# FFN1 a batch later and in groups of 512 tokens, with u through DRAM, in a fused attention and squared-ReLU FFN kernel

## The chip, the cores and the metric

The kernel runs on one core of one Trainium2 chip. The metric is the device time of one execution in microseconds. Three runs of the kernel before took 1504.96, 1505.45 and 1505.6 us; the median, 1505.45 us, is the time that the change is measured against.

## The reference

Attention over 8 batches of 12 heads, with RMS-normed q and k, feeds a two-layer feed-forward network (FFN). All of it is float32 at the interface; w_in and w_out arrive as float64.

```python
q_n, k_n = rmsnorm(q, g_q), rmsnorm(k, g_k)          # q, k, v: 8 x 12 x 448 x 64
scores = (q_n @ k_n.T) / 8
attn = softmax(scores)
x = (attn @ v)                                       # laid out as 3584 tokens x 768
h = x @ w_in                                         # 768 x 2048
r = max(h, 0)
out = (s * r * r + b) @ w_out                        # 2048 x 768
```

A float32 product of full accuracy is made on TensorE out of float32r parts: a number is split into a high part (what float32r keeps) and the rest, and three products high*high, high*low and low*high are added in PSUM.

## The kernel before

**Work and slots.** Two heads make a pair, 48 pairs in all, 6 to a batch. Attention is laid out over 384 slots, 8 to a pair: slot s makes the transposed scores of chunk s (`score_t`: two matmuls, L406 and L409), the exponentials of the same chunk (ScalarE), the plain scores of chunk s + 10 (`score`, L368) with their maximum (`maximum`, L379, VectorE), and the product with the values of chunk s - 2 (`weigh`, L465). A negative slot number is the run-in: the program begins at slot -22. Everything else hangs on the slots in a table, `jobs`: `at(s, f, ...)` puts a step into slot s. Inside a slot every engine gets its instructions in the order of the code, and each engine works through its own list in order. So the table sets the order, and a late instruction holds back all that stands behind it on its engine. SyncE (SP) issues all DMAs, in order too, and a DMA that must wait holds back those behind it.

**Two ways to prepare a pair.** The 6 pairs of batch 0 come in by rows: `load_rows`, `norm_rows` (ScalarE squares, L234 on VectorE sums, GpSimd makes the inverse root, L238, and scales the rows, L239), `turn` (TensorE transposes into PSUM, L246) and `split_turned` (three copies on ScalarE, two subtractions on VectorE, L258 and L259). The other 42 pairs come in already transposed (`load_kq`), and the inverse roots go through DRAM (`load`, `norm`, `keep`, `spread`); `scale` and `split_kq` then take 2 GpSimd multiplications or subtractions of 64 or 128 partitions more per half pair (L330, L352, L353) and L310 and L331 on VectorE. Pairs below `NV` (12) take the value product in plain float32 (one matmul, two passes in the trace); the others split the exponentials (`split_e`, ScalarE; `split_e_lo`, L446, VectorE) and take three float32r matmuls, or two for the last chunk of four.

**After a pair.** `take` copies the product out, `gather` (DMA) collects the row sums, `invert` (VectorE, L488) inverts them, `divide` steps 1 and 2 spread them through DRAM, and step 3 multiplies on GpSimd (L506) into u, at slot 8p + 18 for pair p. Six u tiles stay in SBUF until the batch is whole.

**FFN1.** w_in is converted from float64 in 24 pieces of 128 x 512 (`convert`: L126, L129, L131 and L134 on VectorE, L127 and L137 on ScalarE, L140 on GpSimd). `PACE` starts them at slots -18, -14, -10, -6, -2, 2 and then every fifth slot up to 91. From slot 61 on the `filler` puts 6 FFN1 matmuls into each slot, between the attention's own: 16 blocks of 128 features x 18 matmuls of 448 tokens for each batch (`ffn_in`, L181). Every 48 slots the next batch begins, and just before that `split_x` splits its six u tiles into x, two in each of three slots (L514 on ScalarE, L515 on VectorE). The x tiles are single, so the split has to wait until the last block of the batch before has read them. The relu goes to DRAM (`r_d`). Batches 0 to 6 are filled into the attention; batch 7 runs after it, at the head of the end part, beside the conversion of w_out (32 pieces, VectorE and ScalarE).

**FFN2.** The end part squares r, splits it and runs 28 tiles of 128 tokens x 96 matmuls of 384 columns (`ffn_out`, L706). Its first three tiles take turns while w_out is still being converted.

## Time and profile before

| what | value |
|---|---|
| median of three runs | 1505.45 us |
| the profiled execution: span | 1504.4 us |
| the three runs: lowest and highest | 1504.96 and 1505.6 us |
| TensorE clock granted, mean | 0.988 |
| instructions in the span | 21397 |
| bytes moved by DMA | 230.83 MB |

The span of the profiled execution, from the first to the last instruction, is 1.05 us under the median of the runs; sums are made against the span, and 1.05 us is added at the end. In the lines of the profile PE is TensorE's matmuls and PEld its weight loads, DVE is VectorE, ACT ScalarE, POOL GpSimd, SPq the DMA issues of SyncE. An entry as `ph<-x,wih` reads: writes tile ph, reads x and wih (buffer numbers left out). A group's line ends in busy us, mean ns of one instruction, and the engine's idle time just before such instructions with what ended it.

### The profile page before, as it was taken

Reading aid. Unit: us, or ns where it says so; the run is one execution under the profiler, and the core shown is the slowest. Engines: PE = TensorE matmul, PEld = TensorE weight load, DVE = VectorE, ACT = ScalarE, POOL = GpSimd, SP = SyncE. Lnnn points to the kernel's source line nnn. Section 1 sums busy time; section 2 is a strip of 40 time slices with the busy share of each in tenths; the row PEclk is TensorE's granted clock in tenths of the full one; section 3 lists DMA queues with packets and bytes.
Section 4 is the critical chain, followed back from the end, with each engine's and each line's share of the span. In section 5 each row is a group of like instructions: output and inputs, shape, how many; then the busy total and the mean of one; then the engine's idle time right before and its main releaser. Section 6 shows DMA issues by size and latency. Waiting matters only on the chain.

```text
span 1504.4 us, 21397 instructions
## 1 busy us (share of the span) xinstructions
PE 1452.9 (97%) x7344; PEld 1330.3 (88%) x7344; DVE 874.7 (58%) x1319; ACT 786.3 (52%) x1436; POOL 689.9 (46%) x569
## 2 busy tenths in 40 slices
PE   6887899999999999999999999999999999999998
PEld 6555688899899889889989989999999999999998
DVE  6998876766766676676676665289532222222210
ACT  3675555766766766766676676446432222222210
POOL 6589888777677677777777764100000000000000
PEclk8898999999999999999999999999999999999999
DMA  4468776566566666666656652188333233223200
GB/s 140 110 180 230 214 234 190 167 198 193 175 196 190 193 175 194 191 190 191 183 168 195 191 173 91 67 295 255 113 105 78 80 101 90 78 87 100 84 22 32
DMA packets 221916, 230.83 MB, mean 153 GB/s; under 512 B 78896, under 2 KB 199728, under 8 KB 221808
## 3 DMA queue, kind: packets, MB, share of 16 engines
q1 hardware_dynamic: 221808, 229.47, 51.8%
q8 instruction: 58, 0.95, 0.3%
q14 instruction: 50, 0.41, 0.1%
HBM read 177.21 MB, written 40.84 MB: 145 GB/s over the span
## 4 chain that ended last, share of the span: by engine, by line
PE 88%; DVE 5%; DMA 3%; issue 1%; ACT 1%; POOL 1%; SPq 0%; DVEq 0%; POOLq 0%; ACTq 0%
PE po L706 31%; PE ph L181 30%; PE av L465 13%; PE st L406 4%; PE st L409 4%; PE sh L368 4%; DVE x L515 2%; PE warmth L272 1%; DVE nmx L379 1%; DMA zt<-uz 1%; DMA z_d<-zt 1%; DMA rb<-i_d 0%; DVE al L446 0%; DVE wai L134 0%; DVE wai L129 0%
## 5 line engine op out<-in xcount | busy, mean ns | idle before, releaser
L181 PE MATMUL ph<-x,wih 128*128 128x448 f32 x1536 | 490.9, 367 | 2.6 <-DVE x L515 2.2
L181 PEld LDWEIGHTS ph<-x,wih 128*128 128x128 f32 x1536 | 289.0, 188 | 33.6 <-issue 6.4
L379 DVE TENSOR_REDUCE nmx<-sh 112x1 fp32r<-112x448 f32 x384 | 236.6, 619 | 136.0 <-PE sh L368 130.9
L181 PE MATMUL ph<-x,wil 128*128 128x448 f32 x768 | 294.1, 383 | 0.0
L425 ACT ACTIVATE st<-st 128x448 f32<-128x448 f32 (+1 forms) x288 | 151.1, 525 | 220.8 <-PE st L409 204.2
L706 PE MATMUL po<-woh,gh 128*128 128x384 f32 x896 | 228.0, 334 | 0.0
L706 PE MATMUL po<-wol,gh 128*128 128x384 f32 x896 | 228.0, 334 | 0.0
L706 PE MATMUL po<-woh,gl 128*128 128x384 f32 x896 | 227.7, 334 | 0.0
L368 PE MATMUL sh<-ka,qa 128*112 128x448 f32 x384 | 147.1, 385 | 30.5 <-ACT wih L137 12.5
L465 PE MATMUL av<-ah,vs 128*128 128x448 f32 x576 | 164.3, 366 | 0.1
L406 PE MATMUL st<-qa,ka 128*128 128x448 f32 (+1 forms) x384 | 163.5, 426 | 0.5 <-ACT e L421 0.5
L706 PEld LDWEIGHTS po<-woh,gh 128*128 128x128 f32 x896 | 161.7, 188 | 0.4 <-ACT r L198 0.3
L706 PEld LDWEIGHTS po<-wol,gh 128*128 128x128 f32 x896 | 161.8, 188 | 0.0
L706 PEld LDWEIGHTS po<-woh,gl 128*128 128x128 f32 x896 | 161.8, 188 | 0.0
L181 PEld LDWEIGHTS ph<-x,wil 128*128 128x128 f32 x768 | 144.4, 188 | 17.8 <-issue 6.9
L433 ACT CAST ah<-st 128x448 fp32r<-128x448 f32 (+1 forms) x288 | 154.1, 535 | 1.8
L446 DVE TENSOR_TENSOR al<-st,ah 128x448 fp32r<-128x448 f32 x216 | 132.1, 611 | 35.6 <-ACT ah L433 21.7
L368 PEld LDWEIGHTS sh<-ka,qa 128*112 128x112 f32 x384 | 107.6, 281 | 42.5 <-ACT wih L137 15.8
L688 ACT ACTIVATE r<-r 128x2048 f32<-128x2048 f32 x28 | 53.7, 1919 | 172.9 <-DMA r<-r_d 172.8
L409 PE MATMUL st<-qb,kb 128*128 128x448 f32 (+1 forms) x384 | 141.4, 368 | 0.0
L352 POOL TENSOR_TENSOR ka<-kq,ka 64x448 fp32r<-64x448 f32 x84 | 99.0, 1179 | 91.8 <-ACT ka L349 88.4
L689 DVE TENSOR_SCALAR r<-r,sb_s,sb_b 128x2048 f32<-128x2048 f32 x28 | 37.6, 1345 | 173.0 <-ACT r L688 173.0
(75 smaller groups left out, 2181.2 us busy)
## 6 DMA issues: line engine op xcount, KB each, us to landing
kq<-in_dram SPq DMA_DIRECT2D x84, 448.0 KB, 4.4
rb<-i_d SPq DMA_DIRECT2D x84, 448.0 KB, 5.7
r_d<-r SPq DMA_DIRECT2D x128, 224.0 KB, 2.5
r<-r_d SPq DMA_DIRECT2D x24, 1024.0 KB, 5.9
raw<-in_dram SPq DMA_DIRECT2D x42, 448.0 KB, 5.0
w64i<-in_dram SPq DMA_DIRECT2D x24, 512.0 KB, 4.9
w64o<-in_dram SPq DMA_DIRECT2D x32, 384.0 KB, 5.1
kb<-ka SPq DMA_DIRECT2D x96, 112.0 KB, 3.8
```

What stands on the lines that cost most here:

```text
L181: T.matmul(ph[:, :SEQ], w[:, cc, f0 : f0 + P], xs[b, cc][:, part, :], start=n == 0, stop=n == 3 * NCC - 1,)
L352: G.tensor_tensor(ka[n][D:, a], t[D:, 0], ka[n][D:, a].bitcast(F32), ALU.subtract)
L368: T.matmul(sh[:QC, :SEQ], qa[p % 2][:, a].rearrange("k (p c) -> k c p", c=NQ)[:, c], ka[p % 2][:, a], start=True, stop=True,)
L379: V.tensor_reduce(out=nmxs[p][:, c : c + 1], in_=sh[:QC, :SEQ], op=ALU.max, axis=AX.X, negate=True)
L406: T.matmul(st[:rows, :SEQ], ka[n][:, keys], qa[n][:, q], start=True, stop=False)
L409: T.matmul(st[:rows, :SEQ], kb[n][:, keys], qb[n][:, q], start=False, stop=True,)
L425: S.activation(st[:rows, :SEQ], st[:rows, :SEQ], AF.Exp)
L433: S.copy(ah[:rows], sts[i][0][:rows, :SEQ])
L446: V.tensor_tensor(al, st[:rows, :SEQ], ah[:rows].bitcast(F32), ALU.subtract)
L465: T.matmul(av[:, :SEQ], x, a, start=kc == 0 and m == 0, stop=kc == 3 and m == len(todo) - 1,)
L688: S.activation(r, r, AF.Square)
L706: T.matmul(po[e][0][:, :HALF], x[:, fc, :], w[:, f, e * HALF : (e + 1) * HALF], start=fc == 0 and m == 0, stop=fc == NFC - 1 and m == 2,)
```

## The change

1. **FFN1 begins a batch later and in groups.** `START` goes from 13 to 109, so that the first filler stands in slot 109 instead of 61. The 3584 tokens are cut in 7 groups of 512 instead of 8 batches of 448; a group is again 16 x 18 matmuls, of 512 columns, over 48 slots. Groups 0 to 5 and 36 matmuls of group 6 are filled in (the slot loop now runs to slot 402), the other 252 are done at the head of the end part.
2. **u goes through DRAM.** A group spans two batches, so each u is written out (`keep_u`, one slot after the division) and read back in 512-token pieces (`load_u`, one or two DMAs), two slots before its split. `split_x` now splits one piece in each of six slots. u tiles go from 6 to 2.
3. **End blocks side by side.** The first two and the last two of a group's 16 blocks are made together, piece by piece of x (two PSUM banks held at once), so that a group needs piece c only in its c-th slot and lets go of it six slots before the next group needs it.
4. **w_in is converted thinly**: nothing before slot 0, then one piece every sixth slot, slots 0 to 142.
5. **13 pairs by rows and in plain float32** (`TURNED`) instead of 6 by rows and 12 in float32. The inputs are laid out for it on the host.
6. The second warm-up of 30 matmuls (slot -18) goes. In the end part the low half of a w_out piece follows 2 rounds after the piece instead of 4, with 6 buffers for 10, and a tile of r is always one DMA.

```diff
-START = 13
+START = 109
-PACE = (-18, -14, -10, -6, -2, 2, *range(6, 92, 5))
+PACE = range(0, 144, 6)
+TURNED = 13
...
-    NV = 2 * NP
+    NV = TURNED
+    GT = 512
+    NG = NT // GT
+    GSLOT = NFC * NCC * 3 // sum(FILL)
...
+    def ffn_in(xs, g, fcs):
+        phs = [psum(f"ph{g}_{fc}") for fc in fcs]
         for cc in range(NCC):
+            for (ph, bank), fc in zip(phs, fcs):
+                i, f0 = divmod(fc * P, FS)
+                for m, (w, part) in enumerate(((whi[i], 0), (wlo[i], 0), (whi[i], 1))):
+                    T.matmul(
+                        ph,
+                        w[:, cc, f0 : f0 + P],
+                        xs[g, cc][:, part, :],
...
+    def ffn_in_group(xs, g):
+        pairs = ((0, 1), *((fc,) for fc in range(2, NFC - 2)), (NFC - 2, NFC - 1))
+        return chain.from_iterable(ffn_in(xs, g, fcs) for fcs in pairs)
...
-                u = us[p] = ap.tile([P, SEQ], F32, tag="u", bufs=NP, name=f"u{p}")
+                u = us[p] = ap.tile([P, SEQ], F32, tag="u", bufs=2, name=f"u{p}")
...
+        def keep_u(p):
+            nc.sync.dma_start(u_d[p // NP][p % NP], us.pop(p))
+        def load_u(g, c):
+            u = vxs[g, c] = ap.tile([P, GT], F32, tag="vx", bufs=2, name=f"vx{g}_{c}")
...
+                nc.sync.dma_start(u[:, o : o + n], u_d[b][c][:, off : off + n])
...
+        def split_x(g, c):
+            u = vxs.pop((g, c))
+            x = xs[g, c] = xp.tile([P, 2, GT], F32R, tag=f"x{c}", name=f"x{g}_{c}")
+            S.copy(x[:, 0, :], u)
+            V.tensor_tensor(x[:, 1, :], u, x[:, 0, :].bitcast(F32), ALU.subtract)
...
-            if p >= NP:
+            if p >= TURNED:
...
+            at(s0 + 19, keep_u, p)
-        for b in range(B):
-            for k_ in range(3):
-                at(W * NP * (b + 1) + START - 2 + k_, split_x, b, k_)
-        for _ in range(2):
-            at(FIRST + 1, load_piece)
+        for g in range(NG):
+            for c in range(NCC):
+                at(START + GSLOT * g - 5 + c, load_u, g, c)
+                at(START + GSLOT * g - 3 + c, split_x, g, c)
+        for s_ in (-6, -3):
+            at(s_, load_piece)
...
-            for s_ in range(FIRST, NSLOT + START + 1):
+            for s_ in range(FIRST, START + GSLOT * (NG - 1) + NCC):
...
-                if s_ in (FIRST, FIRST + 4):
+                if s_ == FIRST:
                     warm_up(30)
...
-                b, m = divmod(s_ + 1 - START, W * NP)
-                if m == 0 and b > 0:
+                g, m = divmod(s_ + 1 - START, GSLOT)
+                if m == 0 and g >= 0:
                     filler(None)
-                    units = [(b - 1, fc) for fc in range(NFC)]
-                    fill = chain.from_iterable(ffn_in(xs, *u) for u in units) if b < B else iter(())
+                    fill = ffn_in_group(xs, g)
...
-                    return op.tile([P, WO], I32, tag="wa", bufs=10, name=f"wao{i}")
+                    return op.tile([P, WO], I32, tag="wa", bufs=6, name=f"wao{i}")
...
-        later_by = NFC // NS
+        later_by = 2
...
-                if m < NFC:
-                    for _ in ffn_in(xs, *units[m]):
-                        pass
+                for _ in islice(fill, NCC * 3):
+                    pass
```

The next rows are VectorE's order where FFN1 passes from one batch, or group, to the next (slots 107 to 109 before, 154 to 157 after). x1_c is piece c of the next batch or group, al and ah the low parts of the exponentials that `weigh` waits for, nmx the maxima.

Before:

```order
L515 TENSOR_TENSOR x1_0_2885<-u6_1812,x1_0_2885 128x448
L515 TENSOR_TENSOR x1_1_2888<-u7_2017,x1_1_2888 128x448
L446 TENSOR_TENSOR al106_2895<-st106_2842,ah106_2878 128x448
L379 TENSOR_REDUCE nmx14_2753<-sh117_2891 112x1
L515 TENSOR_TENSOR x1_2_2914<-u8_2221,x1_2_2914 128x448
L515 TENSOR_TENSOR x1_3_2917<-u9_2424,x1_3_2917 128x448
L446 TENSOR_TENSOR ah107_2908<-st107_2873,ah107_2908 64x448
L379 TENSOR_REDUCE nmx14_2753<-sh118_2920 112x1
L310 TENSOR_REDUCE ssq17_2940<-raw17_2804 128x14
L331 SCALAR_TENSOR_TENSOR kq15_1_2827<-kq15_1_2827,gqk_200,rb15_1_2829 128x448
L515 TENSOR_TENSOR x1_4_2950<-u10_2627,x1_4_2950 128x448
L515 TENSOR_TENSOR x1_5_2953<-u11_2851,x1_5_2953 128x448
```

After:

```order
L538 TENSOR_TENSOR x1_0_4011<-vx1_0_3954,x1_0_4011 128x512
L456 TENSOR_TENSOR al153_4021<-st153_3968,ah153_4001 128x448
L389 TENSOR_REDUCE nmx20_3900<-sh164_4017 112x1
L538 TENSOR_TENSOR x1_1_4042<-vx1_1_3982,x1_1_4042 128x512
L456 TENSOR_TENSOR al154_4052<-st154_3996,ah154_4035 128x448
L389 TENSOR_REDUCE nmx20_3900<-sh165_4048 112x1
L538 TENSOR_TENSOR x1_2_4071<-vx1_2_4014,x1_2_4071 128x512
L456 TENSOR_TENSOR ah155_4065<-st155_4030,ah155_4065 64x448
L389 TENSOR_REDUCE nmx20_3900<-sh166_4077 112x1
L320 TENSOR_REDUCE ssq23_4100<-raw23_3952 128x14
L341 SCALAR_TENSOR_TENSOR kq21_1_3978<-kq21_1_3978,gqk_247,rb21_1_3980 128x448
L538 TENSOR_TENSOR x1_3_4111<-vx1_3_4045,x1_3_4111 128x512
```

Before, the six splits stand two by two between the low parts of three slots; after, there is one split of 512 columns to a slot, with one low part and one maximum between them.

The second place is the beginning of VectorE's list, in the run-in. wai is a w_in piece in conversion, tk the transposed rows of a half pair, sh its scores.

Before:

```order
L234 TENSOR_REDUCE ssq0_0_252<-sq0_0_248 112x8
L126 TENSOR_SCALAR wai0_289<-w64i0_244 128x512
L129 SCALAR_TENSOR_TENSOR wai0_289<-w64i0_244,wai0_289 128x512
L131 SCALAR_TENSOR_TENSOR wai0_289<-w64i0_244,wai0_289 128x512
L134 SCALAR_TENSOR_TENSOR wai0_289<-wih0_242,wai0_289 128x512
L234 TENSOR_REDUCE ssq0_1_299<-sq0_1_294 112x8
L126 TENSOR_SCALAR wai1_309<-w64i1_246 128x512
L129 SCALAR_TENSOR_TENSOR wai1_309<-w64i1_246,wai1_309 128x512
L131 SCALAR_TENSOR_TENSOR wai1_309<-w64i1_246,wai1_309 128x512
L134 SCALAR_TENSOR_TENSOR wai1_309<-wih0_242,wai1_309 128x512
L258 TENSOR_TENSOR ka0_184<-tk0_0_0_313,ka0_184 64x448
L259 SCALAR_TENSOR_TENSOR qb0_190<-tk0_0_1_318,gqk_200,qa0_186 64x448
```

After:

```order
L244 TENSOR_REDUCE ssq0_0_293<-sq0_0_289 112x8
L244 TENSOR_REDUCE ssq0_1_303<-sq0_1_299 112x8
L268 TENSOR_TENSOR ka0_231<-tk0_0_0_309,ka0_231 64x448
L269 SCALAR_TENSOR_TENSOR qb0_237<-tk0_0_1_314,gqk_247,qa0_233 64x448
L244 TENSOR_REDUCE ssq1_0_328<-sq1_0_322 112x8
L389 TENSOR_REDUCE nmx0_337<-sh0_335 112x1
L389 TENSOR_REDUCE nmx0_337<-sh1_349 112x1
L389 TENSOR_REDUCE nmx0_337<-sh2_359 112x1
L268 TENSOR_TENSOR ka0_231<-tk0_1_0_339,ka0_231 64x448
L269 SCALAR_TENSOR_TENSOR qb0_237<-tk0_1_1_344,gqk_247,qa0_233 64x448
L244 TENSOR_REDUCE ssq1_1_364<-sq1_1_355 112x8
L389 TENSOR_REDUCE nmx0_337<-sh3_366 112x1
```

Before, eight conversion instructions stand ahead of the first subtraction of transposed keys (L258), and more follow between the maxima; after, none stands there, and the first conversion comes behind the eleventh maximum.

The third place is SyncE's list in the opening, where the row sums of pair 1 are collected (zt1). kb and qb are parts of the next pairs' keys and queries, vf its values, rows a later pair, z_d and zb the inverted sums on their way through DRAM.

Before:

```order
L482 DMA zt1_757<-uz1_0_755 64x1x7
L498 DMA zb0_795<-z_d0_82 64x448 x2
L223 DMA rows5_1_803<-in_2_dram 112x512
L216 DMA raw6_805<-in_1_dram 128x896
L356 DMA qb1_191<-nmx3_764 1x112x4
L356 DMA kb1_189<-ka1_185 64x448
L482 DMA zt1_757<-uz1_1_841 64x1x7
```

After:

```order
L492 DMA zt1_720<-uz1_0_718 64x1x7
L128 DMA w64i4_746<-in_5_dram 128x1024
L508 DMA zb0_758<-z_d0_129 64x448 x2
L233 DMA rows5_1_766<-in_2_dram 112x512
L366 DMA qb1_238<-nmx3_725 1x112x4
L366 DMA kb1_236<-ka1_232 64x448
L519 DMA u_d0_0_81<-u0_795 128x448
L492 DMA zt1_720<-uz1_1_798 64x1x7
```

After, the store of u0 (which waits for GpSimd's multiplication) stands just ahead of the second collection of row sums, for which VectorE's inversion waits two slots later; before, nothing of GpSimd stands between the two.

69 lines of the change are left out of this document (27 added, 42 removed).

## The prediction

> **What bounds the kernel now.** I read the page first, then busy times by stretch, the groups of the opening, and the timeline at the run-in and at a batch border. The page:
>
> ```profile
> span 1504.4 us, 21397 instructions
> PE 1452.9 (97%) x7344; PEld 1330.3 (88%) x7344; DVE 874.7 (58%) x1319; ACT 786.3 (52%) x1436; POOL 689.9 (46%) x569
> PE   6887899999999999999999999999999999999998
> ```
>
> TensorE is full from the fifth slice on and not before. The stretches below are cut at the starts of slots 0, 16, 32 and 56 (an opening without filler), of 64 and 96 (float32 values, with filler), of 104, 112 and 120 (the first of these two holds a batch border), and at the starts of the end part and of FFN2. The columns are us, then busy us (instructions) of PE, PEld, DVE, ACT and POOL, the granted clock, DMA share and GB/s.
>
> ```profile
> 0.00:37.03 37.03, 24.75 (x163) 22.93 (x164) 23.80 (x38) 14.93 (x25) 25.66 (x32) 0.83 0.49 142
> 37.03:71.12 34.09, 27.87 (x110) 19.66 (x108) 31.13 (x47) 21.08 (x41) 19.93 (x21) 0.88 0.39 104
> 71.12:100.39 29.27, 26.79 (x114) 18.35 (x113) 27.00 (x46) 23.54 (x46) 24.78 (x25) 1.00 0.62 159
> 100.39:151.09 50.70, 39.56 (x122) 25.60 (x121) 44.89 (x62) 28.11 (x55) 46.48 (x41) 0.90 0.81 227
> 172.88:255.02 82.14, 82.14 (x354) 66.85 (x352) 59.79 (x81) 43.94 (x85) 68.25 (x57) 1.00 0.73 213
> 274.62:296.40 21.78, 19.93 (x96) 17.36 (x95) 16.41 (x27) 15.94 (x34) 15.28 (x11) 1.00 0.53 166
> 296.40:315.54 19.14, 19.14 (x95) 17.59 (x94) 12.66 (x21) 13.21 (x28) 14.13 (x12) 1.00 0.68 200
> 975.20:1033.57 58.37, 58.37 (x290) 54.10 (x288) 50.80 (x106) 32.38 (x55) 0.00 (x0) 1.00 0.80 265
> 1033.57:1504.40 470.83, 466.39 (x2689) 465.75 (x2687) 137.56 (x144) 122.70 (x112) 0.00 (x0) 1.00 0.30 89
> ```
>
> With filler TensorE alone sets the time: 8 slots of 94 matmuls take 19.14 us, 203.7 ns each. Without it a slot takes 34.09/16 = 2.13, 29.27/16 = 1.83, then 50.70/24 = 2.11 us: in the first two VectorE is busy 91 and 92% of the time, in the third GpSimd 92%. So the sum has three kinds of term: matmuls that are packed, an opening that VectorE or GpSimd paces, and holes.
>
> **FFN1's matmuls: almost nothing.** 2304 of 448 columns become 2016 of 512, the same number of columns. Spacing is 58.37/289 = 202 ns at 448 and 466.39/2689 = 173.4 ns at 384, 0.447 ns a column; drawn on to 512 that is 230.6, in proportion 230.9. A matmul has next to no fixed price to save (1 us in all at most). In the slots I scale 203.7 to 232.8 ns.
>
> **The opening grows from 61 slots (0 to 60) to 109 (0 to 108), and becomes cheaper by the slot.** These groups cover slots 0 to 31; the last two rows are of the whole run.
>
> ```profile
> L379 DVE TENSOR_REDUCE nmx<-sh 112x1 fp32r<-112x448 f32 x32 | 19.2, 614 | 3.2 <-PE sh L368 3.2
> L131 DVE SCALAR_TENSOR_TENSOR wai<-w64i,wai 128x512 int32<-128x512 int32 x7 | 7.0, 998 | 0.0
> L129 DVE SCALAR_TENSOR_TENSOR wai<-w64i,wai 128x512 int32<-128x512 int32 x7 | 6.8, 973 | 0.2
> L134 DVE SCALAR_TENSOR_TENSOR wai<-wih,wai 128x512 f32<-128x512 f32 x7 | 6.6, 938 | 0.0
> L259 DVE SCALAR_TENSOR_TENSOR qb<-tk,gqk,qa 64x448 fp32r<-64x448 f32 x8 | 5.4, 676 | 0.9 <-ACT qa L256 0.6
> L258 DVE TENSOR_TENSOR ka<-tk,ka 64x448 fp32r<-64x448 f32 x8 | 4.9, 618 | 0.4 <-ACT ka L254 0.2
> L234 DVE TENSOR_REDUCE ssq<-sq 112x8 f32<-112x512 f32 x7 | 4.7, 674 | 0.1
> L126 DVE TENSOR_SCALAR wai<-w64i 128x512 int32<-128x512 int32 x7 | 4.4, 634 | 0.0
> L310 DVE TENSOR_REDUCE ssq<-raw 128x14 f32<-128x896 f32 x2 | 2.2, 1086 | 0.2
> L238 POOL TENSOR_TENSOR ri<-ri,mhalf 112x8 f32<-112x8 f32 x8 | 13.9, 1734 | 0.7
> L246 PE MATMUL tk<-ident,rows 112*64 112x112 f32 x96 | 13.5, 292 | 0.0
> L515 DVE TENSOR_TENSOR x<-u,x 128x448 fp32r<-128x448 f32 x48 | 39.6, 867 | 27.7 <-ACT x L514 27.7
> ```
>
> VectorE was busy 31.13 + 27.00 = 58.1 us in these 32 slots. A w_in piece costs it 634 + 973 + 998 + 938 ns = 3.54 us; one in six slots makes 5.3 pieces here instead of 7, -5.9 us. The two sums of the other preparation (L310) go, -2.2, and one sum by rows (L234) comes, +0.7: 50.7 us, 1.58 us a slot. At the same 92% that is 1.72; the lowest it can be is TensorE's own need. That is three matmuls at 0.204, the float32 values at 82.14/32 - 9 x 0.204 = 0.73 and 16 transposes a pair at 13.5/96 = 0.14 (0.28 a slot): 1.62. I add 0.03 for SyncE: the new store of u waits there for GpSimd, and behind it stands the collection of row sums that VectorE's inversion needs two slots later. So slots 0 to 87, which prepare pairs by rows, take 88 x 1.75 = 154 us. From slot 89 on pairs come by the long way again, as they did in slots 32 to 55, with fewer conversions: 21 x 2.0 = 42 us (2.11 at most). Opening: 196 us.
>
> A longer stretch without filler is a longer stretch in which TensorE may fall to half clock: the granted clock above is 0.83, 0.88, 1.00, 0.90 and then 1.00. "TensorE: Matmul & The Clock Gate" of the Trainium skill ("What's actually happening") has the clock at half by default and again after an idle window of about 3.4 us, which speaks against the change; a whole opening at half clock would by that rule need 3.2 us a slot, 157 us more than I take. The trace answers it: slots 16 to 31, whose load the new opening has, kept 1.00; at 0.90 TensorE's 1.62 would be 1.80, and I count that in the range.
>
> **The run-in: 37.0 becomes 24.5 us.** From the timeline:
>
> ```profile
> 2.29 16.24 PE L272 MATMUL warmth<-ident 128*128 128x128 f32 x120 [2.29 <-POOL ident masks.py:199]
> 18.37 0.93 PE L246 MATMUL tk<-ident,rows 112*64 112x112 f32 x8
> 26.75 0.70 PE L368 MATMUL sh<-ka,qa 128*112 128x448 f32 x1 [3.99 <-ACT wih L137]
> 34.66 0.70 PE L368 MATMUL sh<-ka,qa 128*112 128x448 f32 x1 [4.59 <-ACT wih L137]
> 8.39 1.43 POOL L239 TENSOR_TENSOR rows<-rows,ri 112x512 f32<-112x512 f32 x1
> ```
>
> The first transposes stand at 18.37 behind 60 warm-ups, though their rows are scaled at 9.8. Half the warm-ups, at 0.135 us each record, are 8.1 us: 10.3 (11.7 if the clock comes up as late as now). From there to slot 0 took 18.7 us, with 8.6 of waiting for conversions that now come later: 10 us remain. Nor can it be quicker than VectorE's list: 4 maxima, a sum and two subtractions in four slots, 4.4 us, 14.4 in 13 slots, of which the first few start early. 21 to 29; I take 24.5.
>
> **The borders.** A border cost 21.78 - 19.14 = 2.64 us, six times, and the first one about 3:
>
> ```profile
> 284.32 2.25 DVE L515 TENSOR_TENSOR x<-u,x 128x448 fp32r<-128x448 f32 x2 [3.16 <-ACT x L514]
> 287.15 0.47 PE L465 MATMUL av<-al,vs 128*128 128x448 f32 x1 [0.96 <-DVE al L446]
> ```
>
> Two splits (2.25 us) stand ahead of the low part that TensorE waits for. Now one split, 0.867 x 512/448 = 0.99 us, stands there in a slot of 6 x 0.233 + 5.75 x 0.204 = 2.57 us. VectorE has 12.66/8 = 1.58 there, so 2.57: just full for six slots, with one slot of slack. I take 0.4 us a border, 3 in all. Until slot 142 conversions come on top (0.59 a slot; with the splits spread over 48 slots 2.3 of 2.57): 1 us. ScalarE, at 13.21/8 = 1.65, gets longer relus and has room. The change adds a wait here: ScalarE waits for a piece of u to be read back, and behind that wait stand the next exponentials, which TensorE's value products need. What hides it are the two slots (5.1 us) between load and split:
>
> ```profile
> r_d<-r SPq DMA_DIRECT2D x128, 224.0 KB, 2.5
> vr<-in_dram SPq DMA_DIRECT2D x36, 256.0 KB, 3.0
> L514 ACT CAST x<-u 128x448 fp32r<-128x448 f32 x48 | 25.0, 564 | 0.3
> 961.66 0.53 ACT L474 COPY uz<-av 128x448 f32<-128x448 f32 x1 [0.73 <-PE av L465]
> 972.31 2.65 POOL L506 TENSOR_TENSOR u<-uz,zb 64x448 f32<-64x448 f32 x2 [9.96 <-DMA zb<-z_d]
> ```
>
> Read by its nearest row (256 KB in 3.0 us), a load fits. The store and the load of a group's last piece are 2.5 + 3.0 us, and the store is issued two slots ahead of that load. After the last pair the whole way counts: 13.3 us from its last copy-out to the end of u, as now (the last two rows), 5.5 for the new way and 0.6 + 1.0 for the split make 20.4; TensorE has 16 slots of 6 x 0.231 = 1.39 us, 22.2. Without that 1.8 us of cover, each us that the way takes longer is a us of the total, once.
>
> **The end.** 252 matmuls at 231 ns are 58.2 us, as long as 288 at 202. w_out's conversion, beside them, keeps VectorE busy 50.80 of 58.37 us and is not longer than now (the shorter distance of the low halves and the fewer buffers move work in it, they add none), so FFN2 starts without a hole, as now; if it came later, FFN2 would by as much, 0 to 2 us. 470.8 us.
>
> **Sum.** Run-in 24.5, opening 196, FFN1 2016 x 0.2328 = 469.3 and attention beside it 275 x 5.75 x 0.2037 = 322.1, holes 4, FFN2 470.8: 1486.7 us of span, and 1.05 to the median: 1488. The same sum for before, from the start of its first FFN1 matmul, is 160.5 + 469.3 + 35 x 1.345 + 288 x 1.171 + holes 19 + 470.8 = 1503.9, against 1504.4:
>
> ```profile
> 160.50 0.47 PE L181 MATMUL ph<-x,wih 128*128 128x448 f32 x1
> ```
>
> So run-in and opening go from 160.5 to 220.5 us, 60 more for 48 slots more, and the rest, which has 48 slots of attention less and no holes, goes from 1343.9 to 1266.2, 78 less.
>
> **Rivals.**
> 1. *The opening keeps the pace of slots 32 to 55*, 2.11 us, because SyncE's store waits for GpSimd and holds the row sums, and VectorE with them. For: that stretch, with GpSimd at 92%. Against: rows need less of GpSimd (24.78/29.27 in slots 16 to 31). 88 x 0.36 = 32: 1520, slower. It turns slower from a pace of 1.95. 15%.
> 2. *The way through DRAM is late at each border* and ScalarE, then TensorE, waits as long as now: 7 x 2.64 less the 4 counted is 14: 1502, at the edge. For: vx has two buffers, and a load waits for the split two before. Against: 3.0 us of 5.1. 10%.
> 3. *Conversions collide with GpSimd's rows.* One L129 lasted 2.66 us, against 0.69 undisturbed:
>
> ```profile
> 63.51 2.66 DVE L129 SCALAR_TENSOR_TENSOR wai<-w64i,wai 128x512 int32<-128x512 int32 x1
> 73.94 0.69 DVE L129 SCALAR_TENSOR_TENSOR wai<-w64i,wai 128x512 int32<-128x512 int32 x1
> ```
>
> If all three such steps of a piece took 2.66, a piece is 8.6 us, VectorE's need (50.7 + 5.3 x 5.1)/32 = 2.43 a slot: 60 us more, 1548. Against: the means above. 5%. "SBUF — State Buffer" of the Trainium skill ("Who interferes with whom") says why: a VectorE instruction with two SBUF inputs and one of GpSimd share a port that one of them holds to its end. The trace agrees with 0.69 against 2.66.
>
> **How the numbers follow.** The forecast, 70%, has its own range of 1474 to 1502: paces of 1.62 and 1.85 (-11, +9), the run-in (-3.5, +4.5). About 0.2%, 3 us, can be told from no change. Faster by more: the forecast nearly whole and half of rival 2, 0.74; slower, beyond 1508.5: most of rivals 1 and 3, 0.18; the same, 0.08. The range takes in rival 2 and the nearer part of rival 1 (pace 2.0): 1472 to 1512.
>
> **What would show it.** Right: slot 0 near 24.5 us, the first FFN1 matmul near 221, a slot with filler 2.57 us, spacing 231 ns in the end part, no hole over 1 us at borders. Wrong: a first FFN1 matmul after 238 us, with VectorE waiting for row sums or SyncE for u; ScalarE waiting for vx; a 512-column matmul away from 231 ns.

## The result and the profile after

The changed kernel takes 1525.59 us (median of 4 runs, 1523.02 to 1529.0) against 1505.53 us for the kernel before (1504.96 to 1506.51): a ratio of 1.0135, with a 95% interval of 1.0119 to 1.0151. It is slower by 20 us; the forecast was 1488 us, 17 us of gain, with 1472 to 1512 us held open. The profiled execution has a span of 1523.1 us. The page, the three lines that answer those shown of before:

```profile
span 1523.1 us, 21036 instructions
PE 1456.9 (96%) x7102; PEld 1283.9 (84%) x7102; DVE 853.1 (56%) x1326; ACT 791.3 (52%) x1426; POOL 651.5 (43%) x556
PEclk9999998999999999999999999999999999999999
```

TensorE still is the engine that is full, and the clock stands at full speed in nearly every slice. So the loss is in places, not in a new general bound. The busy times by stretch find the places: the run-in, the whole opening of slots 0 to 103, then of it pair 3 and pair 4, the eight slots of pair 13 with the first border, a pair with filler and no border, a pair with a border, the end part before FFN2.

```profile
0.00:22.37 22.37, 15.08 (x103) 13.94 (x103) 11.30 (x20) 9.69 (x16) 17.72 (x28) 1.00 0.31 86
22.37:218.43 196.06, 171.10 (x694) 117.92 (x692) 161.51 (x268) 136.07 (x264) 145.89 (x145) 0.97 0.57 160
65.70:79.40 13.70, 13.00 (x58) 9.22 (x57) 11.18 (x20) 10.75 (x21) 10.06 (x12) 1.00 0.51 143
79.40:96.05 16.65, 13.32 (x58) 9.22 (x57) 14.83 (x27) 10.35 (x20) 11.86 (x13) 1.00 0.59 166
218.43:251.67 33.24, 19.54 (x65) 14.09 (x64) 24.37 (x37) 17.34 (x36) 23.89 (x20) 0.79 0.68 206
292.55:312.93 20.38, 20.38 (x96) 17.80 (x95) 16.19 (x26) 14.48 (x30) 16.27 (x13) 1.00 0.79 231
353.67:378.45 24.78, 21.55 (x95) 17.54 (x94) 14.89 (x24) 15.99 (x33) 14.91 (x12) 1.00 0.76 221
994.60:1052.21 57.61, 57.47 (x253) 47.15 (x252) 48.11 (x101) 32.69 (x57) 0.00 (x0) 1.00 0.83 274
```

A pair with filler takes 20.38 us, 2.547 a slot, and TensorE is busy in all of it. A pair with a border takes 24.78, so that border costs 4.4 us; the five later borders cost 4.4, 5.7, 3.9, 5.0 and 4.2, and 0.9 falls into the pair behind the last. Pair 13 takes 33.24 us, with TensorE busy in 19.54 of them and the clock at 0.79. FFN2 begins at 1052.21 us. Two of the signs of being wrong that the prediction named are there: the first FFN1 matmul stands at 241.28 us, where 221 was said and 238 was the limit, and ScalarE waits for vx. Set beside the sum on record, span for span:

| Part | Forecast, us | Measured, us | Difference |
|---|---|---|---|
| run-in, to slot 0 | 24.5 | 22.4 | -2.1 |
| slots 0 to 103 (88 x 1.75 + 16 x 2.0) | 186.0 | 196.1 | +10.1 |
| slots 104 to 111 (5 x 2.0 + 3 x 2.57 + 0.4) | 18.1 | 33.2 | +15.1 |
| slot 112 to the end of FFN1 (what is left of the sum) | 787.3 | 800.5 | +13.2 |
| FFN2 | 470.8 | 470.9 | +0.1 |
| span | 1486.7 | 1523.1 | +36.4 |

The fourth row holds 22 us more at five borders (24.1 where 2 were taken), and 9 less elsewhere, of which 5.8 are 272 slots at 2.547 instead of 2.568.

One border from close by. The first group is SyncE's list in the timeline, with the issue of two pieces of u (vx) and of two transfers of the preparation; then ScalarE's splits, VectorE's second split with the low part that follows it, and the matmul that TensorE stood before longest:

```profile
356.38 0.90 SPq L531 DMA_DIRECT2D vx<-u_d  x2
357.38 0.60 SPq L276 DMA_DIRECT2D kq<-in_dram  x1
358.04 0.59 SPq L336 DMA_DIRECT2D rb<-i_d  x1
358.68 1.18 SPq L531 DMA_DIRECT2D vx<-u_d  x2
361.56 0.62 ACT L537 CAST x<-vx 128x512 fp32r<-128x512 f32 x1 [1.29 <-DMA vx<-u_d]
365.90 0.62 ACT L537 CAST x<-vx 128x512 fp32r<-128x512 f32 x1 [1.92 <-DMA vx<-u_d]
366.56 0.69 DVE L538 TENSOR_TENSOR x<-vx,x 128x512 fp32r<-128x512 f32 x1 [2.59 <-ACT x L537]
367.17 0.62 DVE L456 TENSOR_TENSOR al<-st,ah 128x448 fp32r<-128x448 f32 x1
367.84 0.47 PE L475 MATMUL av<-al,vs 128*128 128x448 f32 x1 [1.48 <-DVE al L456]
```

The piece issued at 358.68 was split at 365.90, 7 us on. ScalarE stood ready for these two pieces 3.9 and 5.3 us after their issue (361.56 - 1.29 - 356.38 and 365.90 - 1.92 - 358.68), so of the 5.1 us of cover the first had 3.9 and the second all, and it did not suffice. ScalarE waited 1.92 us for it, VectorE 2.59 us for ScalarE, and TensorE 1.48 us for the low part that stood behind the split in VectorE's list. The same three engines in the waits of the whole run (total us, times, longest), two of SyncE's waits, and from the view of the tile vx how long a load took to land:

```profile
DVE x L538 <- ACT x L537: 70.6, 29, 10.8
ACT x L537 <- DMA vx<-u_d: 36.9, 19, 5.9
PE av L475 <- DVE al L456: 24.2, 18, 6.3
SPq L531 <- DVE x L538: 40.1, 27, 3.3
SPq L519 <- POOL u L516: 37.1, 18, 4.4
DMA to landing us min/median/max: 1.6/3.0/8.1
```

The median of 3.0 us is what the prediction had taken from its nearest row; the 8.1 us it had not reckoned with. Of ScalarE's 36.9 us, 17.6 fall at the five later borders, and all but one of these 11 waits are for the first two pieces of a group.

### The profile page after: what moved, and what is told of

The parts are those of the page before. It is cut to its first block, busy times and chain, and to the rows that moved or that the text cites. A ratio compares the mean times of both kernels' runs of the same rounds, so it can differ in the third digit from the quotient of the medians.

```text
span 1523.1 us, 21036 instructions
## 1 busy us (share of the span) xinstructions
PE 1456.9 (96%) x7102; PEld 1283.9 (84%) x7102; DVE 853.1 (56%) x1326; ACT 791.3 (52%) x1426; POOL 651.5 (43%) x556
## 4 chain that ended last, share of the span: by engine, by line
PE 75%; DMA 7%; DVE 6%; issue 4%; POOL 3%; ACT 3%; SPq 1%; POOLq 0%; ACTq 0%; DVEq 0%
PE po L722 30%; PE ph L188 21%; PE av L475 11%; PE sh L378 4%; PE st L416 4%; PE st L419 4%; DMA vx<-u_d 3%; DMA w64o<-in_dram 1%; POOL ri L324 1%; DMA rb<-i_d 1%; PE tk L256 1%; DVE x L538 1%; DMA zt<-uz 1%; SPq L531 1%; DVE nmx L389 1%
## 5 line engine op out<-in xcount | busy, mean ns | idle before, releaser
L188 PE MATMUL ph<-x,wih 128*128 128x512 f32 x1344 | 466.1, 394 | 0.3
L188 PEld LDWEIGHTS ph<-x,wih 128*128 128x128 f32 x1344 | 253.4, 189 | 28.5 <-ACT x L537 2.0
L435 ACT ACTIVATE st<-st 128x448 f32<-128x448 f32 (+1 forms) x280 | 146.9, 525 | 233.3 <-PE st L419 227.0
L188 PE MATMUL ph<-x,wil 128*128 128x512 f32 x672 | 265.3, 395 | 0.0
L416 PE MATMUL st<-qa,ka 128*128 128x448 f32 (+1 forms) x384 | 176.9, 461 | 2.0 <-DVE nmx L389 1.4
L475 PE MATMUL av<-ah,vs 128*128 128x448 f32 x560 | 159.0, 365 | 5.1 <-DVE al L456 5.1
L443 ACT CAST ah<-st 128x448 fp32r<-128x448 f32 (+1 forms) x280 | 149.4, 534 | 1.8
L516 POOL TENSOR_TENSOR u<-uz,zb 64x448 f32<-64x448 f32 x96 | 117.8, 1227 | 47.9 <-DMA zb<-z_d 44.5
L188 PEld LDWEIGHTS ph<-x,wil 128*128 128x128 f32 x672 | 126.8, 189 | 12.1
L475 PEld LDWEIGHTS av<-ah,vs 128*128 128x128 f32 x560 | 105.6, 189 | 32.2 <-DVE al L456 5.9
```

The costliest lines, as they stand in the source:

```text
L188: T.matmul(ph, w[:, cc, f0 : f0 + P], xs[g, cc][:, part, :], start=cc == 0 and m == 0, stop=cc == NCC - 1 and m == 2,)
L416: T.matmul(st[:rows, :SEQ], ka[n][:, keys], qa[n][:, q], start=True, stop=False)
L435: S.activation(st[:rows, :SEQ], st[:rows, :SEQ], AF.Exp)
L443: S.copy(ah[:rows], sts[i][0][:rows, :SEQ])
L475: T.matmul(av[:, :SEQ], x, a, start=kc == 0 and m == 0, stop=kc == 3 and m == len(todo) - 1,)
L516: G.tensor_tensor(u[a], uzs.pop((p, j))[a], zb[a], ALU.mult)
```

## The experiments

The first theory: the read-back of u is late at the borders, because a load waits for the split that frees one of two buffers (the wait of 40.1 us), and ScalarE's wait then holds the exponentials. Its rivals: the split itself fills VectorE; SyncE's store of u; the conversions of w_in; transfers that stand in each other's way. Ratios are to the kernel before, with their 95% intervals; the ratio of the change is 1.0135.

| Run | What it is | us | Ratio |
|---|---|---|---|
| e1 | changed kernel, no reading back | 1505.66 | 1.0006 (0.9996 to 1.0015) |
| e2 | changed, three buffers for vx | 1524.91 | 1.0136 (1.0121 to 1.0152) |
| e3 | changed, store of u a slot later | 1520.92 | 1.0105 (1.009 to 1.012) |
| e4 | before, run-in of the change | 1496.25 | 0.9941 (0.9926 to 0.9956) |
| e5 | e1, splits spread | 1496.86 | 0.994 (0.9924 to 0.9957) |
| e6 | changed, conversions pause | 1523.82 | 1.0118 (1.0099 to 1.0137) |
| e7 | changed, u read back early | 1508.8 | 1.0027 (1.0017 to 1.0037) |
| e8 | e4, end blocks side by side | 1485.92 | 0.9865 (0.985 to 0.988) |
| e9 | changed, with e3, e7 and spread splits | 1501.21 | 0.9981 (0.9971 to 0.9991) |
| e11 | e9, first border relieved | 1491.62 | 0.9911 (0.9896 to 0.9926) |
| e10 | e8, 9 pairs by rows | 1483.31 | 0.9861 (0.9846 to 0.9876) |
| e12 | e10, first splits early | 1501.08 | 0.9986 (0.9977 to 0.9995) |
| e13 | e12, those splits three slots later | 1476.43 | 0.981 (0.9796 to 0.9823) |

### What a border costs

**e1, without the reading back.**

```diff
-            u = vxs[g, c] = ap.tile([P, GT], F32, tag="vx", bufs=2, name=f"vx{g}_{c}")
...
+            u = vxs[0] = ap.tile([P, GT], F32, name="vx0")
...
-            u = vxs.pop((g, c))
+            u = vxs[0]
...
-                at(START + GSLOT * g - 5 + c, load_u, g, c)
...
+        at(40, load_u, 0, 0)
```

> This kernel leaves out the loading of u from DRAM ahead of each group: every split reads one tile that was loaded once at slot 40, so FFN1's input is wrong while its instructions stay. Theory (the read-back is late: ScalarE waits for vx and holds the exponentials, and SyncE, which waits for the split that frees one of two buffers, issues the next load late): the borders lose their holes, about 35 us in seven of them, and keep at most 0.5 us each, so 1525.5 - 32 = 1493 us, with 1488 to 1499 held open. Rival (the split itself, 0.99 us on VectorE and a piece on ScalarE in a slot that is full, takes the time): borders keep 4 us or more each, 1515 us or more. Both leave slots 0 to 103 at about 196 us.

It took 1505.66 us, 20 less than the change and not the 32 that were expected. A pair with a later border:

```profile
477.65:500.07 22.42, 21.03 (x95) 17.69 (x94) 14.92 (x24) 16.02 (x33) 15.20 (x12) 1.00 0.57 177
```

Each later border fell to 2.04 us (22.42 us for the pair, where a pair without a border has 20.38), and pair 13 became shorter by 2 us only. So the read-back was about 60% of the later borders (14 of 24 us). What else there was shows in VectorE's timeline at this border:

```profile
492.27 1.08 DVE L320 TENSOR_REDUCE ssq<-raw 128x14 f32<-128x896 f32 x1
493.26 0.89 DVE L341 SCALAR_TENSOR_TENSOR kq<-kq,gqk,rb 128x448 f32<-128x448 f32 x1
494.07 1.64 DVE L533 TENSOR_TENSOR x<-vx,x 128x512 fp32r<-128x512 f32 x1
495.64 0.61 DVE L456 TENSOR_TENSOR al<-st,ah 128x448 fp32r<-128x448 f32 x1
496.17 0.61 DVE L389 TENSOR_REDUCE nmx<-sh 112x1 fp32r<-112x448 f32 x1
```

These five are one slot's work and take 4.83 us of a slot of 2.55. In every eighth slot the sum of squares and the scaling of the next pairs fall together, and the fourth split of a group stood in just that slot. It took 1.64 us there, beside GpSimd's own scaling (L340, from 493.62 us on for 1.54), where others take 0.69.

**e5, the six splits out of that slot**, in the kernel without the reading back:

```diff
-                at(START + GSLOT * g - 3 + c, split_x, g, c)
+                at(START + GSLOT * g + (-5, -4, -3, -1, 1, 2)[c], split_x, g, c)
```

> The kernel without the reading back of u (every split reads one tile loaded once, so FFN1's input is wrong), and the six splits of a group moved from six slots in a row to the slots -5, -4, -3, -1, 1 and 2 from the group's start. Theory (without the read-back a border still costs 2.0 us, because in one slot of eight VectorE has a sum of squares, a scaling, the inversion, a low part and a maximum already, and a split makes 4.85 us of a slot of 2.55): without a split in that slot the borders from the second on fall from 2.0 to 0.5 us or less, 1505.7 - 9 = 1497 us (1494 to 1500). Rival (two blocks side by side end together, and their two rectifications on ScalarE, or the splits as such, hold TensorE): borders keep 1.5 us or more, 1502 us or more.

1496.86 us, as the theory had it. A pair with a border, by busy times:

```profile
470.63:491.64 21.01, 20.74 (x95) 17.77 (x94) 14.19 (x24) 15.77 (x33) 15.59 (x12) 1.00 0.64 189
```

21.01 less 20.38 is 0.63 us a border. The side-by-side blocks and the splits as such cost 0.63 us where the prediction had 0.4; the pile in one slot cost 1.4 us more, and the reading back 2 to 4.

**e2, a third buffer**, for which one of the two buffers of u was given up:

```diff
-                u = us[p] = ap.tile([P, SEQ], F32, tag="u", bufs=2, name=f"u{p}")
+                u = us[p] = ap.tile([P, SEQ], F32, tag="u", bufs=1, name=f"u{p}")
...
-            u = vxs[g, c] = ap.tile([P, GT], F32, tag="vx", bufs=2, name=f"vx{g}_{c}")
+            u = vxs[g, c] = ap.tile([P, GT], F32, tag="vx", bufs=3, name=f"vx{g}_{c}")
```

> One change to the changed kernel: u is read back into three buffers instead of two (paid for by one buffer of u instead of two). Theory (a load stands behind the split two pieces before it, of the very same slot): the load is then freed by a split one slot earlier, so about half of the 35 us of border holes go, 1508 us (1500 to 1514). Rival (loads are late whatever the buffers, since SyncE is behind with other issues or the transfers are slow): 1521 us or more.

No change: 1524.91 us. ScalarE's wait for vx went from 36.9 to 33.6 us only, and at the five later borders from 17.6 to 16.9. The view of the tile vx in this run has:

```profile
DMA to landing us min/median/max: 1.8/4.5/7.5
```

The median time to land rose from 3.0 to 4.5 us: pieces that were issued earlier stood in the queue longer, though some still landed 1 to 2 us earlier than before. None of this mattered, because the late pieces are the first two of a group, and these find a free buffer with two buffers as with three: at the border shown above they were issued at 356.12 and 358.40 us in this run and took 5.3 and 7.2 us to land, as they had taken 4.9 and 7.0. So the wait of 40.1 us for a free buffer, though it was real, was not what made u late. That part of the first theory fell. What stands ahead of a piece in the queue is seen in the timeline above: between two pieces lie a kq and an rb, 448 KB each.

**e7, the pieces read back as soon as they are stored**, from the second group on, into six buffers, four of them in the room of w_in's raw pieces (the last piece excepted, which is loaded where it was):

```diff
...
-                at(START + GSLOT * g - 5 + c, load_u, g, c)
+                early = (0, 8, 26, 28, 32, 39)[c] - 39
+                at(START + GSLOT * g + (early if g else c - 5), load_u, g, c)
```

> One change to the changed kernel: from the second group on each piece of u is read back as soon as it is stored (the last piece excepted, which is loaded where it was), into six buffers, four of them in the room of w_in's raw pieces, which are done by then. Three buffers had changed nothing, so theory now: the loads are late because they are issued in the same slots as 448 KB transfers of the preparation and stand behind them in the queue. Then the borders from the second on fall from 5.4 to the 2.0 us of the kernel without reading back: 1525.5 - 15 = 1511 us (1507 to 1515). Rival (the read-back costs by the traffic and by SyncE's issues themselves, wherever they stand): 1519 us or more.

1508.8 us. A border costs what it did with no reading back at all, 22.41 us for the pair against 22.42:

```profile
353.16:375.57 22.41, 21.02 (x95) 17.70 (x94) 14.95 (x24) 15.99 (x33) 15.27 (x12) 1.00 0.64 194
```

The same bytes and the same issues cost the borders nothing when they are issued eight slots or more ahead of their split (all but the last piece). So neither the traffic nor SyncE's work was the price; the two slots between load and split were, in a stretch where other transfers are queued. That these are the kq, rb and raw transfers is read from the timeline; they were not taken away singly. The six buffers of this run came with the early loads and were not tried alone, but a third buffer had changed nothing.

**e8, the same border without a reading back by design**: the kernel before, u in SBUF and groups of one batch, with the change's run-in (e4, below), its end blocks side by side, and one split a slot outside the full one.

```diff
...
-            for k_ in range(3):
-                at(W * NP * (b + 1) + START - 2 + k_, split_x, b, k_)
+            for c in range(NCC):
+                off = (-5, -4, -3, -1, 1, 2)[c]
+                at(W * NP * (b + 1) + START + (off if b < B - 1 else min(off, 0)), split_x, b, c)
...
```

> The kernel before with the change's run-in (as in the run of the run-in alone, 1496 us) and its end blocks side by side, with u taken from SBUF and FFN1 in batches of 448 tokens as before; one split a slot, none of them in the slot that VectorE has full. Theory (a border of one split a slot is nearly free where nothing has to be read back): the borders fall from 2.64 to about 0.5 us, six of them, and the first by 1 us, 1496.3 - 13 = 1483 us (1479 to 1488). Rival (side by side moves the wait to ScalarE's rectifications or to the banks): 1491 us or more.

1485.92 us, 10 less than with the run-in alone. A pair with a border, which takes 21.78 us in the kernel before:

```profile
380.98:401.00 20.02, 19.67 (x95) 17.35 (x94) 15.01 (x24) 15.36 (x34) 15.35 (x12) 1.00 0.64 187
```

A border costs 0.88 us instead of 2.64. So the part of the change that was to help at borders does help where u need not come from DRAM and no split stands in the full slot; the two were not separated in this kernel.

### The opening and the run-in

**e3, the store of u one slot later**, behind the collection of row sums:

```diff
-            at(s0 + 19, keep_u, p)
+            at(s0 + 20, keep_u, p)
```

> One change to the changed kernel: the store of u stands one slot later, behind the collection of row sums instead of ahead of it. Theory (the store waits for GpSimd on SyncE and holds the row sums, VectorE and so TensorE, in every third pair of the opening): pairs 4 and 7 fall from 2.08 to about 1.73 us a slot and slots 0 to 103 from 196 to about 187 us; total about 1517 us (1513 to 1521). Rival (those pairs are slow because w_in's conversions, six slots apart, fall on the preparation of pairs, eight slots apart): slots 0 to 103 stay at 194 to 197 us and the total at 1522 to 1530.

1520.92 us: 4.7 less, half of what was expected, at the edge of the theory's range. Slots 0 to 103:

```profile
22.25:214.48 192.23, 172.20 (x693) 118.75 (x692) 163.75 (x268) 134.71 (x262) 145.67 (x144) 0.96 0.57 162
```

192.2 us where the change has 196.1. Pairs 4 and 7 fell from 2.08 to 2.01 us a slot only, and pair 9 from 2.05 to 1.82. In the five other runs that keep the store where the change has it, these slots take 194.8 to 195.7 us, and in e9 and e11, which move it as well, 190.6 and 191.7, so the store accounts for 4 of the 10 us. Why every third pair keeps 2.0 was not tried by itself, but the two rows of pairs 3 and 4 shown above point at a reason. Four conversions take the 24 slots of three pairs, and they do not fall evenly: by VectorE's groups pair 4 holds eight conversion instructions (6.6 us), pair 3 only four (2.9 us). Hence 14.83 us of VectorE's work there instead of 11.18. At the prediction's own 92% these 14.83 us would take 16.1, which is what pair 4 has in e3 (16.05).

**e4, the run-in alone**, in the kernel before:

```diff
-PACE = (-18, -14, -10, -6, -2, 2, *range(6, 92, 5))
+PACE = range(0, 96, 4)
...
-        for _ in range(2):
-            at(FIRST + 1, load_piece)
+        for s_ in (-6, -3):
+            at(s_, load_piece)
...
-                if s_ in (FIRST, FIRST + 4):
+                if s_ == FIRST:
```

> The kernel before with the run-in of the change alone: one set of warm-up matmuls instead of two, the first two pieces of w_in loaded 6 and 3 slots ahead of slot 0, and 24 conversions every four slots from slot 0 instead of from slot -18. Theory (the run-in's gain has nothing to do with the rest of the change): slot 0 moves from 37.0 to about 23 us, the opening takes 1 to 3 us more, total about 1493 us (1489 to 1498). Rival (the conversions that are moved into the opening fill VectorE there, 6.4 pieces of 3.54 us, and give the gain back): 1502 us or more.

1496.25 us, 0.6% faster than before. The stretch from slot 0 to slot 64:

```profile
22.84:159.16 136.32, 111.19 (x399) 72.94 (x398) 130.46 (x189) 89.71 (x172) 117.20 (x101) 0.95 0.69 198
```

Slot 0 stands at 22.84 instead of 37.03, 14.2 us earlier, as it does in the changed kernel (22.37). Slot 64 is reached at 159.16 instead of 172.88, 13.7 earlier, so nearly all of it lasts in the profiled execution. That one is the fastest of the four; by the medians the gain is 8.2 us (1504.44 us for the kernel before, run beside it).

**e10, 9 pairs by rows** instead of 6, in the kernel with the mended borders:

```diff
+TURNED = 9
...
-            if p >= NP:
+            if p >= TURNED:
...
```

> The kernel before with the change's run-in and its end blocks side by side (1485.9 us), and 9 pairs prepared by rows instead of 6. Theory (a pair by rows paces an opening without filler at 1.73 us a slot where the long way needs 2.0 to 2.3): pairs 4 to 7, 18.3 us each but the last with the first border in it, fall to 14.5 or 15, which takes 8 us away or a little more, and three pairs' transposes, 2.25 us each on TensorE, cost nothing where it waits: 1478 us (1474 to 1482). Rival (conversions every four slots instead of every six fill VectorE, so that rows, which need more of VectorE, give nothing): 1484 us or more.

1483.31 us, between what was expected (1478) and the rival's 1484; the interval of its ratio overlaps that of e8, so the gain is not shown. Pair 6 fell from 2.28 to 1.90 us a slot, but pairs 3 and 4 rose from 1.89 and 1.92 to 2.02. VectorE has the conversions every four slots there, and its busy share shows it:

```profile
22.52:135.52 113.00, 94.94 (x390) 65.25 (x388) 106.57 (x167) 79.77 (x153) 84.09 (x80) 0.97 0.54 149
```

94% for VectorE: what rows save on GpSimd is worth little where VectorE is the pace.

### The first border

**e6, a pause of the conversions** from slot 101 to 113:

```diff
-PACE = range(0, 144, 6)
+PACE = (*range(0, 102, 6), *range(114, 142, 4))
```

> One change to the changed kernel: the conversions of w_in pause from slot 101 to 113 and the last seven come every four slots from 114. Theory (the first border loses 13 us to VectorE, which has two conversions there beside splits and the preparation by the long way): pair 13 falls from 4.16 to about 3.3 us a slot and the total by about 6 us, to 1519 us (1515 to 1522). Rival (it is the change from preparation by rows to the long way, with transfers that come late and steps of VectorE and GpSimd that hold each other, whatever the conversions do): 1523 us or more.

1523.82 us, not to be told from the change. Pair 13 fell by 3.3 us, to 29.9, and pair 14 became 1.2 us longer. The conversions alone are not the cause.

**e9, the three mends together** (e7, the spread splits of e5, e3):

```diff
-            at(s0 + 19, keep_u, p)
+            at(s0 + 20, keep_u, p)
...
-                at(START + GSLOT * g - 5 + c, load_u, g, c)
-                at(START + GSLOT * g - 3 + c, split_x, g, c)
+                early = (0, 8, 26, 28, 32, 39)[c] - 39
+                at(START + GSLOT * g + (early if g else (-7, -6, -5, -3, -2, 0)[c]), load_u, g, c)
+                at(START + GSLOT * g + (-5, -4, -3, -1, 1, 2)[c], split_x, g, c)
```

> The changed kernel with three mends that were found singly: u read back early from the second group on (1508.8 us alone), the six splits of a group out of the slot that VectorE has full (worth 8.8 us in the kernel without the reading back), the store of u behind the collection of row sums (worth 4.6 us alone). Theory (the three are separate losses at separate places): they add up, 1508.8 - 8.8 - 4.6 = 1495 us (1492 to 1499). Rival (they share one loss, and the splits that now come later wait for ScalarE or for the last piece, which is still loaded where it was): 1501 us or more.

1501.21 us, where 1495 were expected. The later borders have 0.64 us each, so that mend holds (the pair behind the first of them has 1.3 more), and slot 104 comes at 213.15 us. But pair 13 has 34.01 us, 1.5 more than in e7, with the clock at 0.80:

```profile
213.15:247.16 34.01, 20.44 (x66) 14.31 (x64) 23.85 (x37) 17.89 (x37) 23.39 (x21) 0.80 0.67 204
```

Here the first group is still read back two slots ahead of its splits. In e5, with the same splits and no reading back (and the store of u where the change has it), pair 13 takes 27.98 us, 6 less. So the read-back does cost the first border something, which e1 (2 us) did not show while the splits stood in a row.

**e11, the first border relieved as well**: the pause of e6, and the first group's pieces (no earlier group holds x then) read back and split one by one as they come, eight slots apart, but for the last.

```diff
-PACE = range(0, 144, 6)
+PACE = (*range(0, 102, 6), *range(114, 142, 4))
...
-                early = (0, 8, 26, 28, 32, 39)[c] - 39
-                at(START + GSLOT * g + (early if g else (-7, -6, -5, -3, -2, 0)[c]), load_u, g, c)
-                at(START + GSLOT * g + (-5, -4, -3, -1, 1, 2)[c], split_x, g, c)
+                early = (0, 8, 26, 28, 32, 39)[c] if g else (0, 8, 16, 24, 32, 39)[c]
+                off = (-5, -4, -3, -1, 1, 2)[c] if g or c == 5 else 8 * c - 35
+                at(START + GSLOT * g + early - 39, load_u, g, c)
+                at(START + GSLOT * g + off, split_x, g, c)
```

> The kernel with the three mends, and in the first border three things more: the conversions of w_in pause from slot 101 to 113, and the first group's pieces are read back and split as soon as each is stored, spread over 40 slots, the last one excepted. Theory (the eight slots from 104 take 28 to 33 us instead of the 18 that were forecast because splits, read-back and conversions all fall there on VectorE and ScalarE, which leaves TensorE idle, and the clock that is granted then falls to 0.5): pair 13 takes 21 us or less, total about 1487 us (1484 to 1491). Rival (it is the preparation by the long way, with GpSimd 0.94 to 0.98 busy in pairs 10 and 12 and transfers at 350 GB/s, that has no reserve when FFN1 starts): pair 13 keeps 26 us or more, 1493 us or more.

1491.62 us. Pair 13 went from 34.0 to 23.8 us:

```profile
213.79:237.55 23.76, 18.04 (x65) 13.30 (x64) 15.50 (x25) 14.29 (x31) 20.87 (x21) 0.86 0.77 230
```

That is between the theory's 21 and the rival's 26. VectorE has 15.50 us of work there instead of 23.85. Splits, read-back and conversions that fall together were 10 of the 15 us missing. The span of the profiled execution, the fastest of four, is 1487.4 us, against 1486.7 on record. That the sum comes out so well is partly luck: slots 0 to 103 are still 5.7 us over and pair 13 another 5.7, while the run-in is 2.4 under and the rest of FFN1, whose slots are shorter than forecast, 7.9.

**e12 and e13, the same in the kernel before.** In e10 pair 7 holds the first border and takes 24.57 us. Both runs split the first batch's pieces one by one, eight slots apart; e12 two slots behind GpSimd's step that makes u, e13 five slots behind it.

```diff
-                off = (-5, -4, -3, -1, 1, 2)[c]
+                off = (-5, -4, -3, -1, 1, 2)[c] if b else 8 * c - 41
```

> The kernel before with the run-in, the end blocks side by side and 9 pairs by rows (1483.3 us), and the first batch's six splits done as soon as each piece of u is there, eight slots apart, since no earlier group reads x. Theory (the first border is dear because everything falls on VectorE and ScalarE at once, whichever way u takes): pair 7, 24.6 us with the border in it where 16.4 would be its price by the other slots, loses 3 us or more, and the total goes to 1480 us (1477 to 1482). Rival (there it is the conversions, every four slots, and the preparation that take the time): 1482.5 us or more.

1501.08 us, 18 more instead of 3 less. Pair 7 did fall, to 19.66 us, but the opening rose to 2.6 us a slot. Two rows of the view of the tile x in the opening (us in total, times) and three of the timelines show how:

```profile
  ACT x L519: 23.9, 5
  POOL u L512: 4.7, 5
67.86 0.56 ACT L519 CAST x<-u 128x448 fp32r<-128x448 f32 x1 [0.43 <-POOL u L512]
68.46 0.63 DVE L520 TENSOR_TENSOR x<-u,x 128x448 fp32r<-128x448 f32 x1 [3.89 <-ACT x L519]
72.00 0.70 PE L374 MATMUL sh<-ka,qa 128*112 128x448 f32 x1 [4.73 <-DVE ka L264]
```

ScalarE waited 0.43 us for u at this split, VectorE 3.89 us for ScalarE, and TensorE 4.73 us for the keys behind it in VectorE's list. VectorE sets the pace of the opening and runs ahead of ScalarE; a split makes it wait for ScalarE's place in the order, and ScalarE for GpSimd's. Five waits, 23.9 us.

```diff
-                off = (-5, -4, -3, -1, 1, 2)[c] if b else 8 * c - 41
+                off = (-5, -4, -3, -1, 1, 2)[c] if b else 8 * c - 38
```

> The run with the first batch's splits done early (1501.1 us, 18 us worse where 3 better were expected), with each split three slots later, at five slots behind the step of GpSimd that makes u instead of two, and out of the slots in which VectorE prepares rows. Theory (the splits as such are cheap, and what cost 24 us of the opening was VectorE waiting 3.9 to 5 us at each of five splits for ScalarE, which waited for GpSimd): the opening goes back to 1.9 to 2.0 us a slot, and pair 7 now has what was expected of the earlier run, 3 us less than 24.6: total 1480 us (1477 to 1483). Rival (in an opening that VectorE paces any split costs, wherever it stands): 1488 us or more.

1476.43 us, the fastest of all, 1.9% under the kernel before. The opening is back at 112.88 us, and pair 7 went from 24.57 to 17.87 us, with the clock at 1.00 instead of 0.86. The first row is of e10:

```profile
135.52:160.09 24.57, 17.41 (x60) 12.22 (x59) 19.69 (x31) 14.17 (x28) 18.38 (x15) 0.86 0.61 181
```

```profile
22.80:135.68 112.88, 95.09 (x389) 65.30 (x388) 106.38 (x172) 81.76 (x158) 84.10 (x80) 0.97 0.54 148
135.68:153.55 17.87, 16.02 (x61) 11.24 (x59) 17.17 (x26) 11.91 (x23) 16.81 (x15) 1.00 0.87 253
```

The same splits, three slots later, cost 25 us less. And the first border was dear in this form of the kernel before too, in part for the same reason: taking five of the six splits away from it took 6.7 us.

## Why the prediction was wrong, point by point

- **The borders (failed).** "I take 0.4 us a border, 3 in all" was 24 us at the five later ones. Two things were wrong. The cover, "two slots (5.1 us) between load and split", was set against a median of 3.0 us for a single transfer; at a border, where the first two loads of a group are queued behind 448 KB transfers, up to 7 and 8 us were needed (14 of the 24 us: e1, e7). Two of the five borders, those of 5.7 and 5.0 us, hold a stretch at half clock besides (last section). And VectorE's load was a mean, "1.58 there, so 2.57: just full for six slots". The work is not even over the slots: one in eight has 3.2 us without a split (7 us of the 24: e5). Without both a border cost 0.63. Rival 2 named the mechanism, late reading back, but its reason, the two buffers, was not the cause (e2). It was priced at 2.64 us a border, the price of the old ones; there was no reason for that bound, and 10% was too little.
- **The first border (failed).** Slots 104 to 108 were counted at 2.0 us, as openings by the long way go, and the border with them at 0.4. They took 15 us more than the sum. The trace of before held the warning in its own first border: from its first FFN1 matmul at 160.50 us to slot 64 at 172.88 it has 12.4 us, where three slots with filler are 7.7, and I put "about 3" for the difference. Of the 15 us, 10 went when splits, loads and conversions were moved away together (e11); in e13, a form of the kernel before, moving the splits took 6.7 us from its own first border. Singly, pausing the conversions took 3.3 us (e6), leaving out the reading back 2.0, and this with the splits spread 5.3 (e5), while spread splits with the reading back took nothing (e9). So the shares do not simply add; what each is worth, and what holds the last 5 or 6 us, stays open.
- **The opening (half right).** The pace by rows was right in most pairs: 13.70 us for pair 3 is 1.71 a slot, where 1.75 was said. Every third pair has 2.05 to 2.09. "I add 0.03 for SyncE" was the term: the store of u waited 37.1 us for GpSimd, 31.6 of them in slots 0 to 103, and moving it took 4 of the 10 us away (e3). Rival 1 had the mechanism, for all pairs instead of some. The rest is the step "50.7 us, 1.58 us a slot", a mean again: the trace has pairs with twice the conversion work of their neighbours, and the neighbours cannot make up for it, since TensorE's own need (1.62) holds them at 1.71. That this is the cause of the remaining 6 us was not tried in a run of its own.
- **The run-in (right).** 22.4 us for 24.5; the first transposes stand at 10.73 us, where 10.3 was said. In the kernel before slot 0 comes as early (e4).
- **FFN1's matmuls and the end (right).** A slot with filler is 2.547 us for 2.568. 252 matmuls at the end took 57.6 us, 229 ns each, where 58.2 were said, and FFN2 followed without a hole.
- **Rival 3 (not the case in the opening).** Single steps did collide, but the price of a piece stayed below what was taken: 6.6 us for the two of pair 4, 3.3 each, where the sum had 3.54. At the borders the collision was seen in the split (1.64 us for 0.69, e1). "SBUF — State Buffer" of the Trainium skill ("Who interferes with whom") says that a VectorE instruction with two SBUF inputs and one of GpSimd share a port; the split reads two tiles in SBUF, and the trace agrees, with 1.64 us beside GpSimd's scaling against 0.69.
- **The sum as a whole.** Its additions come out. One reading of the page, without effect on it, is off: TensorE is full from the sixth slice on, not from the fifth. And the sum held a warning that was not read. The opening's slots grew from 123.5 to 196 us, 72.5 more; what came behind shrank by 77.7, of which 15 were the holes of the borders. So moving FFN1 a batch later lost 10 us by my own numbers, and the gain was all run-in and borders, which need no such move. The runs agree: with the borders mended, the first one included, the kernel that moves FFN1 has 1491.62 us (0.9896 to 0.9926 of before); the one that does not has 1485.92 (0.985 to 0.988) with run-in and later borders alone, and 1476.43 with its first border mended and 9 pairs by rows.

## What to carry to other kernels

A transfer's cover is to be held against the slowest landing in the stretch where it is issued, with what is queued ahead of it, and not against the median of its kind; where the data are ready long before, load early. A mean load per slot says nothing of a slot in which three steps fall together: list the instructions of the slot into which new work goes. And ask of a sum with several gains which of them needs the expensive part of the change: here the cheap parts alone, in the old order, were the faster kernel.
